# Batch 2's q and k through DMA transposes, on top of a reworked first and second batch, in a fused Nyström attention and MLP kernel

## The chip, the cores and the metric

The kernel runs on one core of one Trainium2 chip. The metric is the device time of one execution in microseconds, lower is better. Batches are numbered from 0, so the "third batch" of the change is batch 2. Unless a run is called slow, all times are of fast runs; a program on one core has no second die to compare with, so a run counts as slow when it lies over 1.5% above the fastest of its kernel.

## The reference

The inputs are q, k and v of 8 batches, 8 heads, 576 positions and 64 channels, and two MLP weights.

```python
q_lm = q.reshape(B, H, 32, 18, D).mean(axis=3)      # landmarks: segment means
k_lm = k.reshape(B, H, 32, 18, D).mean(axis=3)
A, Bm, C = sm(q, k_lm), sm(q_lm, k_lm), sm(q_lm, k) # softmax(a b^T / 8)
Z = Bm^T / (norm_1(Bm) * norm_inf(Bm) + 1e-6)       # per head, schematic
for _ in range(6):
    Z = 2 * Z - Z @ Bm @ Z                          # Newton steps for the inverse
x = A @ Z @ C @ v                                   # then [4608, 512]
out = relu(x @ w_in) ** 2 @ w_out                   # d_ff = 2048
```

## The kernel before

The kernel never forms x. It folds `Z C v` and `w_in` of a batch into one matrix `G`, so that the MLP's first product is `G^T A^T` (`mlp_in`), the second is `mlp_out`. While TensorE works on the MLP of batch b, the attention of batch b+1 is woven into its instruction stream. The order of each engine's instructions is fixed when the program is built.

This kernel's score matmuls read q and k with the channels on the partitions, that is, transposed. Batches below `DMA_T` do it with TensorE (36 transposes of 128 columns, the results then copied out of PSUM), later ones with DMA transposes:

```python
DMA_T = 3

def prepare(b, nms=("k", "q")):                     # cut
    ...
        nc.vector.tensor_copy(X[nm][:], raw)        # "cast": reorders heads and columns
        if b >= DMA_T:
            nc.sync.dma_start_transpose(X[nm + "T"]..., X[nm]...)
    if "k" in nms:
        ...
        if b >= DMA_T:
            nc.sync.dma_start_transpose(X["tT"][:], X["qkt"]...)   # the last 64 rows, "tails"
```

When a batch's cast may run is pinned to a point in the batch before it. For batches 3 to 7 this is the first Newton step of the batch before; for batch 2 it is later, after batch 1's `WT` (k) and the last copy of its `G` (q):

```python
for it in range(3):
    EY, ED, last = joint_step(EY, ED)
    if it == 0 and b > 1:
        X["kpin"] = X["qpin"] = last
...
last = nc.vector.tensor_copy(WT[:], wt[:])
if b == 1:
    X["kpin"] = last
for n in range(4):                                  # G, in four parts
    ...
        last = nc.vector.tensor_copy(dst, gg[:])    # every second part
        if b == 1:
            X["qpin"] = last
```

All loads but those of batch 0's q and k are issued by GpSimd on one queue, in this order: w_in, v of batch 0, q and k of batch 1, w_out, and so on.

The softmax here doesn't subtract the row's maximum and nothing guards it: scores larger than these inputs give would overflow.

Of the kernel before, what the change touches and what calls it, by code (L numbers as in the profile page):

```python
# [8 lines left out]
P = 128  # L9
# [8 lines left out]
H = 8  # L18
S = 576
D = 64  # L20
# [10 lines left out]
DMA_T = 3  # L31
# [3 lines left out]
def kernel(  # L35
# [97 lines left out]
    masked = band(mask4[:], [[32, 4]], 31, -1)  # L133
    blk_bf = const.tile([P, 4, M], BF16, name="blk_bf")
    nc.vector.tensor_copy(blk_bf[:], mask4[:, :].unsqueeze(2).to_broadcast([P, 4, M]))
# [37 lines left out]
    def prepare(b: int, nms=("k", "q")):  # L173

        X = loaded[b]
        for nm in nms:
            X[nm] = loads.tile([P, NC4, H, D], BF16, tag=nm + "nat", bufs=1, name="nat")
            X[nm + "T"] = attn.tile([P, NC4, NPAIR, P], BF16, tag=nm + "T", name="T")
            raw = X[nm + "raw"].rearrange("p h c d -> p c h d")
            if b == 0:  # L180
                for lo, hi in ((0, H // 2), (H // 2, H)) if nm == "q" else ((0, H),):
                    nc.vector.tensor_copy(X[nm][:, 0:2, lo:hi, :], raw[:, 0:2, lo:hi, :])
                    nc.scalar.copy(X[nm][:, 2:4, lo:hi, :], raw[:, 2:4, lo:hi, :])
                continue
# [10 lines left out]
    def warm(n):  # L195

        z = bds[1].rearrange("p a b c -> p (a b c)")
        for _ in range(n):
            nc.tensor.matmul(idle[:, 0:2 * P], lhsT=z[:, 0:P], rhs=z[:, 0:2 * P],
                             start=True, stop=True)  # L200

    def attention(b: int, R: dict):
# [6 lines left out]
        def transposed(nm, half):  # L209
            if not first:  # L210
                tps = ntile([P, 2, NPAIR, P], BF16)[:]
            else:
                tps = psum.tile([P, 4, NPAIR, P], BF16, tag="h", bufs=2, name="tps")[:, 0:2, :, :]
# [20 lines left out]
        def segment_means(ti, nm):  # L234
# [5 lines left out]
            for n, (p, c) in enumerate(order):  # L240
                src = X[nm][:, c, 2 * p:2 * p + 2, :] if c < NC4 else X["qkt"][:, 2 * p:2 * p + 2, :]
                nc.tensor.matmul(  # L242
                    means[:, ti, p, :],
                    lhsT=src.rearrange("p h d -> p (h d)"),
                    rhs=seg[:, c + (ti if c == NC4 else 0), :],
                    start=(n == 0 and (first or ti == 1)), stop=(c == NC4), skip_group_check=True,
                )
# [44 lines left out]
        def stationary(src, tag):  # L292

            if first:
# [3 lines left out]
                nc.vector.tensor_copy(res[:], src)  # L298
# [23 lines left out]
        def inverse_begin():  # L322
# [3 lines left out]
            cs = small.tile([P, 2], F32, tag="cs", name="cs")  # L326
            nc.vector.reduce_sum(cs[:], BB[:, 0, :, :], axis=AX.X)
            rows = small.tile([P, 2, M], F32, tag="rows", name="rows")
            nc.vector.transpose(rows[:], cs[:, :].unsqueeze(2).to_broadcast([P, 2, M]))
# [79 lines left out]
        ras = [small.tile([P, NC4 + 1, 4], F32, tag="ra", name="ra") for i in range(2)]  # L409
        rras = [small.tile([P, NC4 + 1, 4], F32, tag="rra", name="rra") for i in range(2)]  # L410
        parts = ((0, 3), (3, NC4 + 1)) if first else ((0, NC4 + 1),)

        def a_sums(i, part=0):
            lo, hi = parts[part]
            nc.vector.reduce_sum(ras[i][:, lo:hi, :],  # L415
                                 EA[:, i, lo:hi, :].rearrange("p c (h m) -> p c h m", m=M), axis=AX.X)
            if hi == NC4 + 1:
                nc.vector.reciprocal(rras[i][:], ras[i][:])

        def a_rows(i, part=0):  # L420
            lo, hi = parts[part]
# [3 lines left out]
                rras[i][:, lo:hi, :].unsqueeze(3).to_broadcast([P, hi - lo, 4, M]), ALU.mult)  # L425
# [13 lines left out]

        def c_values():  # L440

            cv = ntile([P, 2, D + 1])
            for qd in range(2):
                for c in range(NC4 + 1):
                    for lo, hi in ((0, D), (D, D + 1)):
                        for a in range(4):
                            h = 4 * qd + a
                            lh = EC[:, qd, c, :] if c < NC4 else ect[:, qd, :]
                            rv = (ones_bf[:] if lo else
                                  X["vm"][:, h, c, :] if c < NC4 else X["vt"][:, h, :])  # L450
                            nc.tensor.matmul(  # L451
                                cv[M * a:M * a + M, qd, lo:hi], lhsT=lh[:, M * a:M * a + M], rhs=rv,
                                start=(qd == 0 and c == 0 and lo == 0), stop=(c == NC4),
                                skip_group_check=True)
            rc2 = small.tile([P, 2], F32, tag="rc2", name="rc2")
            nc.vector.reciprocal(rc2[:], cv[:, :, D])
            nc.vector.tensor_tensor(cvb[:], cv[:, :, 0:D],
# [3 lines left out]
        if first:  # L461
            prepare(0, ("k",))
            warm(6)
            k0 = transposed("k", 0)
            k1 = transposed("k", 1)
            load_rest(dve(X["qkt"][:], X["qkt32"][:]))
            dve(*k0)
            act(*k1)
            segment_means(1, "k")
            transposed_tail()  # L470
            prepare(0, ("q",))
            warm(8)
# [3 lines left out]
            dve(*q0)  # L476
            q1 = transposed("q", 1)
            landmark_softmax()
            act(*q1)
            scores("k", 0)  # L480
            BT, ED = inverse_first(*inverse_begin())
# [37 lines left out]
        def aside():  # L519
            for f, *args in side.pop(0):  # L520
                f(*args)
            if first:
                warm(2)
# [215 lines left out]
```

## Time and profile before

| | before |
|---|---|
| median time | 273.28 us (3 runs), 273.21 us with the fourth |
| first MLP matmul | 24.64 us |
| first matmul of G of batch 1 | 51.67 us |
| from there to G of batch 2 | 30.71 us |
| batches after that | 31.37 and 28.16 us in turn |
| batch 2's first q scores | 69.38 us |

The rows of this table come from the timeline view. First the page's busy shares, and three rows of its 40 slices (each slice 6.8 us; a digit is a busy share in tenths; PEclk is the clock granted to TensorE):

```profile
PE 254.2 (94%) x3051; PEld 150.2 (56%) x3051; DVE 174.9 (65%) x497; ACT 157.6 (58%) x274; POOL 42.7 (16%) x66
...
PE   2978799999999999999999999999999999999994
...
PEclk9999999999999999999999999999999999999999
DMA  7999999999699979997599929994821011211032
```

TensorE is full from the sixth slice on. The DMA row is at 7 or 9 for the first ten slices, about 67 us. The windows view with the columns span, busy time of each engine, clock, DMA share and GB/s says the same of TensorE in figures:

```profile
60.00:80.00 20.00, 19.50 (x259) 12.53 (x258) 17.10 (x54) 14.01 (x25) 3.77 (x5) 1.00 1.05 128
100.00:120.00 20.00, 19.90 (x266) 11.07 (x265) 14.34 (x36) 11.36 (x19) 3.42 (x4) 1.00 1.27 148
```

The chain of work that ended last (start, length, what) goes through DMA at the start:

```profile
9.19 7.26 DMA vm<-in_v_dram
16.73 14.90 DMA raw<-in_q_dram
```

The timeline of the kernel before has the first MLP matmul, and batch 2's first q scores, which follow a TensorE transpose and wait for nothing:

```profile
24.64 0.67 PE L601 MATMUL h<-AT,G 128*128 128x288 bf16 x4 [0.30 <-ACT G L579]
...
68.24 0.39 PE L226 MATMUL n<-ident_bf,qkt 128*128 128x128 bf16 x4
...
69.38 0.40 PE L390 MATMUL n<-bd_83,T 128*128 128x64 bf16 x8
```

The view of one tile, asked for the transposed q and k, gives the time of DMA transposes from issue to landing. This is all ten of them, and then the two of batch 7, issued when no load was left in the queues:

```profile
DMA to landing us min/median/max: 5.1/10.7/20.5
...
DMA to landing us min/median/max: 5.1/5.2/5.3
```

In this kernel the same transpose took 5.1 to 5.3 us with no load in the queues and 9.6 to 20.5 us, two to four times as much, in batches 3 to 6, beside loads.

### The profile page before, as it was taken

The page shows a single profiled execution, that of the slowest core. Times are in us where ns is not written, and L with a number is a line of the kernel's source. Part 1 is how long each engine was busy: PE and PEld are TensorE (multiplying, and loading weights), DVE is VectorE, ACT ScalarE, POOL GpSimd, SP SyncE. Part 2 cuts the span into 40 slices and gives each one's busy share as a digit, 9 for nine tenths or more (in the row PEclk, how much of TensorE's full clock was granted, in tenths as well). Part 3 has the DMA queues.
Part 4 walks back from the last instruction along what each step waited for, and adds up shares of the span by engine and source line. Part 5 has one row for each costly group of instructions (what it writes and reads, how often), then busy time and mean ns, then how long its engine had stood idle before and what let it go on. Part 6 is the DMA issues. An engine that isn't in the chain of part 4 may idle for free.

```text
span 270.4 us, 7294 instructions
## 1 busy us (share of the span) xinstructions
PE 254.2 (94%) x3051; PEld 150.2 (56%) x3051; DVE 174.9 (65%) x497; ACT 157.6 (58%) x274; POOL 42.7 (16%) x66
## 2 busy tenths in 40 slices
PE   2978799999999999999999999999999999999994
PEld 1844565466654665556644665466645665466444
DVE  4687788758794569647974669548964859545100
ACT  2555687366935677267926676467836674577211
POOL 3744333310420202202220220200000000000000
PEclk9999999999999999999999999999999999999999
DMA  7999999999699979997599929994821011211032
GB/s 207 229 203 198 203 205 190 209 207 144 83 160 123 186 107 137 199 159 105 113 157 153 177 61 155 174 149 80 176 61 62 18 41 41 78 41 40 19 98 79
DMA packets 69793, 35.34 MB, mean 131 GB/s; under 512 B 37376, under 2 KB 64256, under 8 KB 69760
## 3 DMA queue, kind: packets, MB, share of 16 engines
q0 software_dynamic: 37696, 17.17, 54.5%
q1 hardware_dynamic: 26816, 8.39, 22.4%
q10 hardware_dynamic: 5248, 9.31, 11.3%
q8 instruction: 24, 0.39, 0.6%
q14 instruction: 9, 0.07, 0.1%
HBM read 36.70 MB, written 9.44 MB: 171 GB/s over the span
## 4 chain that ended last, share of the span: by engine, by line
PE 69%; DVE 15%; DMA 10%; ACT 3%; issue 1%; SPq 0%; POOL 0%; DVEq 0%
PE ops L630 21%; PE h L601 16%; PE n L630 9%; DMA raw<-in_q_dram 6%; DVE gT L608 4%; PE g L573 3%; DMA vm<-in_v_dram 3%; DVE ra L415 2%; PE n L314 2%; DMA qkt_94<-in_q_dram 2%; ACT r L607 2%; PE n L451 2%; PE n L242 2%; PE n L390 1%; DVE an L422 1%; PE n L432 1%
## 5 line engine op out<-in xcount | busy, mean ns | idle before, releaser
L607 ACT ACTIVATE r<-h 128x576 bf16<-128x576 f32 x128 | 81.9, 652 | 33.4 <-PE h L601 30.4
L601 PE MATMUL h<-AT,G 128*128 128x288 bf16 x512 | 83.1, 286 | 1.2 <-ACT r L607 0.8
L630 PE MATMUL ops<-w_out_bf,gT 128*128 128x512 bf16 x304 | 83.2, 379 | 0.1
L608 DVE TENSOR_TENSOR gT<-r 128x576 bf16<-128x576 bf16 x128 | 57.4, 452 | 39.2 <-ACT r L607 38.1
L630 PEld LDWEIGHTS <-gT 128*128 128x128 bf16 x592 | 53.6, 98 | 40.5 <-issue 6.4
L601 PEld LDWEIGHTS <-G 128*128 128x128 bf16 x512 | 45.5, 97 | 21.6 <-issue 2.4
L630 PE MATMUL n<-w_out_bf,gT 128*128 128x512 bf16 x112 | 29.6, 380 | 0.0
L587 DVE CAST G<-g 128x1024 bf16<-128x1024 f32 x14 | 17.1, 1225 | 13.2 <-PE g L573 13.2
L585 ACT CAST G<-g 128x1024 bf16<-128x1024 f32 x14 | 14.2, 1012 | 9.5 <-PE g L573 9.1
L639 ACT COPY o_sb<-ops 128x512 f32<-128x512 f32 x19 | 11.1, 585 | 4.5 <-PE ops L630 4.4
L436 ACT COPY AT<-n 128x576 bf16<-128x576 bf16 x9 | 5.7, 638 | 13.5 <-PE n L432 11.1
L314 PEld LDWEIGHTS <-ED 128*128 128x128 bf16 x84 | 6.7, 97 | 12.2 <-DVE ED L305 8.4
L390 PEld LDWEIGHTS <-T 128*128 128x128 bf16 x256 | 11.3, 98 | 3.7
L422 DVE TENSOR_TENSOR an<-EA,rra 128x640 bf16<-128x640 f32 (+2 forms) x18 | 13.3, 740 | 0.0
L415 DVE TENSOR_REDUCE ra<-EA 128x20 f32<-128x640 f32 (+2 forms) x18 | 13.0, 721 | 0.0
L84 POOL DMA_DIRECT2D qkt<-in_k_dram x7 | 4.8, 690 | 46.7 <-PE n L252 30.1
L106 POOL DMA_DIRECT2D vm<-in_v_dram x8 | 7.1, 881 | 32.1 <-PE n L451 27.4
L242 PEld LDWEIGHTS <-nat 128*128 128x128 bf16 x256 | 8.7, 97 | 5.1 <-DVE nat L185 2.3
L96 POOL DMA_DIRECT2D raw<-in_k_dram x7 | 6.6, 936 | 29.3 <-DVE ED L305 18.6
L394 ACT ACTIVATE EA<-n 128x512 f32<-128x512 f32 x16 | 9.7, 607 | 1.8 <-PE n L390 1.8
L185 DVE COPY nat<-raw 128x2048 bf16<-128x2048 bf16 x14 | 9.4, 686 | 1.6 <-DMA raw<-in_q_dram 0.9
L394 ACT ACTIVATE EC<-n 128x512 bf16<-128x512 f32 x16 | 9.7, 604 | 1.2 <-PE n L390 1.1
(185 smaller groups left out, 322.6 us busy)
## 6 DMA issues: line engine op xcount, KB each, us to landing
out_dram<-o_sb ACTq DMA_DIRECT2D x31, 256.0 KB, 4.0
vm<-in_v_dram POOLq DMA_DIRECT2D x8, 512.0 KB, 14.7
raw<-in_k_dram POOLq DMA_DIRECT2D x7, 512.0 KB, 10.5
raw<-in_q_dram POOLq DMA_DIRECT2D x7, 512.0 KB, 13.8
w_in_bf<-in_moe_w_in_dram POOLq DMA_DIRECT2D x4, 512.0 KB, 10.2
w_out_bf<-in_moe_w_out_dram POOLq DMA_DIRECT2D x4, 512.0 KB, 16.2
out_dram<-o_sb ACTq DMA_DIRECT2D x9, 128.0 KB, 2.4
raw<-in_k_dram SPq DMA_DIRECT2D x1, 1024.0 KB, 5.5
```

The source lines that it names most:

```text
L242: nc.tensor.matmul(means[:, ti, p, :], lhsT=src.rearrange("p h d -> p (h d)"), rhs=seg[:, c + (ti if c == NC4 else 0), :], start=(n == 0 a ...
L314: nc.tensor.matmul(res[a:a + w, qd, :], lhsT=diagonal[a:a + w, qd, :], rhs=moving(qd)[a:a + w], start=True, stop=True)
L390: nc.tensor.matmul(sc[:, c, j, :, :], lhsT=X[nm + "T"][:, c, p, :], rhs=BD[:, 1 if nm == "q" else 0, p, 0:64], start=True, stop=True)
L394: nc.scalar.activation((EA if nm == "q" else EC)[:, qd, 0:NC4, :], sc.rearrange("p c j i m -> p c (j i m)"), AF.Exp, scale=SCALE)
L415: nc.vector.reduce_sum(ras[i][:, lo:hi, :], EA[:, i, lo:hi, :].rearrange("p c (h m) -> p c h m", m=M), axis=AX.X)
L422: nc.vector.tensor_tensor(an[:, i, lo:hi, :].rearrange("p c (h m) -> p c h m", m=M), EA[:, i, lo:hi, :].rearrange("p c (h m) -> p c h m", ...
L585: nc.scalar.copy(dst, gg[:])
L587: last = nc.vector.tensor_copy(dst, gg[:])
L601: last = nc.tensor.matmul(h[:, j, 0:HALF], lhsT=G[:, qd, f * P:(f + 1) * P], rhs=AT[:, qd, j * HALF:(j + 1) * HALF], start=(qd == 0), stop ...
L607: nc.scalar.activation(r.rearrange("p (j t) -> p j t", j=2), h[:, :, 0:HALF], AF.Relu)
L608: return nc.vector.tensor_tensor(gT[:, f, o:o + S], r[:], r[:], ALU.mult)
L630: mark[:] = [nc.tensor.matmul(ops, lhsT=gT[:, f, t * P:t * P + P], rhs=w_out_bf[:, f, i * n:i * n + n], start=(f == 0), stop=(f == NF - 1))]
```

## The change

Its intent: start the first MLP matmuls sooner, keep the second batch from blocking them, and relieve TensorE of batch 2's transposes, which the DMA engines do "for free" in all later batches. The diff, cut to its core:

```diff
-DMA_T = 3
+DMA_T = 2
@@ row sums of C: 10 full matmuls instead of 40 column-tiled ones
-                    for lo, hi in ((0, D), (D, D + 1)):
-                        for a in range(4):
-                            ...
+            for qd in range(2):
+                for c in range(NC4 + 1):
+                    nc.tensor.matmul(cv[:, qd, D:D + 1], lhsT=c_of(qd, c), rhs=ones_bf[:],
+                                     start=False, stop=(c == NC4), skip_group_check=True)
@@ first batch (many lines cut): weight loads follow the k cast, q is cast in halves,
@@ k's scores come later, fewer idle matmuls, G's first part is copied in halves
+            load_rest(X["cast"])
+            prepare(0, ("q",), ((0, H // 2),))
-            load_rest(dve(X["qkt"][:], X["qkt32"][:]))
@@ second batch: k transposed with the segment means, steps spread by a table
+            if b == 1:
+                for half, evac in ((0, dve), (1, act)):
+                    evac(*transposed("k", half))
+                    yield
+        early = [0, 0, 0, 0, 0, 0, 1, 2, 3, 3, 4, 5, 7, 9, 12, half]
-            if (b, f) == (0, 2):
-                loaded[0]["qpin"] = square
+            if b == 0 and f in (4, 8):
+                loaded[0][("kpin", "qpin")[f // 8]] = square
                 prepare_next(1)
```

In the built program two orders move that the diff doesn't show. On the load queue, batch 2's v now comes before its k and q. On SyncE, which issues the transposes, batch 3's tail transpose stands before batch 2's k transpose.

More of the change, by code (lines that the diff above doesn't have):

```diff
@@ L133 @@
     masked = band(mask4[:], [[32, 4]], 31, -1)
+    blk = const.tile([P, 4, M], F32, name="blk")
+    nc.vector.tensor_copy(blk[:], mask4[:, :].unsqueeze(2).to_broadcast([P, 4, M]))
     blk_bf = const.tile([P, 4, M], BF16, name="blk_bf")
-    nc.vector.tensor_copy(blk_bf[:], mask4[:, :].unsqueeze(2).to_broadcast([P, 4, M]))
+    nc.vector.tensor_copy(blk_bf[:], blk[:])
     ones_bf = const.tile([P, 1], BF16, name="ones_bf")
@@ L171, in ntile, with prepare @@
         return psum.tile(shape, dt, tag="n", bufs=3, name="n")
-    def prepare(b: int, nms=("k", "q")):
+    def prepare(b: int, nms=("k", "q"), halves=((0, H),)):
         X = loaded[b]
         for nm in nms:
-            X[nm] = loads.tile([P, NC4, H, D], BF16, tag=nm + "nat", bufs=1, name="nat")
-            X[nm + "T"] = attn.tile([P, NC4, NPAIR, P], BF16, tag=nm + "T", name="T")
+            if nm not in X:
+                X[nm] = loads.tile([P, NC4, H, D], BF16, tag=nm + "nat", bufs=1, name="nat")
+                X[nm + "T"] = attn.tile([P, NC4, NPAIR, P], BF16, tag=nm + "T", name="T")
             raw = X[nm + "raw"].rearrange("p h c d -> p c h d")
             if b == 0:
-                for lo, hi in ((0, H // 2), (H // 2, H)) if nm == "q" else ((0, H),):
+                for lo, hi in halves if nm == "q" else ((0, H),):
                     nc.vector.tensor_copy(X[nm][:, 0:2, lo:hi, :], raw[:, 0:2, lo:hi, :])
-                    nc.scalar.copy(X[nm][:, 2:4, lo:hi, :], raw[:, 2:4, lo:hi, :])
+                    X["cast"] = nc.scalar.copy(X[nm][:, 2:4, lo:hi, :], raw[:, 2:4, lo:hi, :])
                 continue
@@ L193, in prepare, with warm, in_turn @@
                 nc.sync.dma_start_transpose(X["tT"][:], X["qkt"].rearrange("p h d -> p (h d)"))
-    def warm(n):
+    def warm(n, width=512):
         z = bds[1].rearrange("p a b c -> p (a b c)")
         for _ in range(n):
-            nc.tensor.matmul(idle[:, 0:2 * P], lhsT=z[:, 0:P], rhs=z[:, 0:2 * P],
+            nc.tensor.matmul(idle[:, 0:width], lhsT=z[:, 0:P], rhs=z[:, 0:width],
                              start=True, stop=True)
+    mark, begin, front = [], [], []
+    def in_turn():
+        return tc.issue_after(front[0].ins) if front else nullcontext()
     def attention(b: int, R: dict):
@@ L212, in transposed @@
             else:
-                tps = psum.tile([P, 4, NPAIR, P], BF16, tag="h", bufs=2, name="tps")[:, 0:2, :, :]
+                if half == 0:
+                    X["tps"] = psum.tile([P, 4, NPAIR, P], BF16, tag="h", bufs=2, name="tps")
+                tps = X["tps"][:, 2 * half:2 * half + 2, :, :]
             for i in range(2):
@@ L239, in segment_means @@
                            (0, x[1] // 2, x))
-            for n, (p, c) in enumerate(order):
-                src = X[nm][:, c, 2 * p:2 * p + 2, :] if c < NC4 else X["qkt"][:, 2 * p:2 * p + 2, :]
-                nc.tensor.matmul(
-                    means[:, ti, p, :],
-                    lhsT=src.rearrange("p h d -> p (h d)"),
-                    rhs=seg[:, c + (ti if c == NC4 else 0), :],
-                    start=(n == 0 and (first or ti == 1)), stop=(c == NC4), skip_group_check=True,
-                )
+            with in_turn() if b == 1 else nullcontext():
+                for n, (p, c) in enumerate(order):
+                    src = X[nm][:, c, 2 * p:2 * p + 2, :] if c < NC4 else X["qkt"][:, 2 * p:2 * p + 2, :]
+                    nc.tensor.matmul(
+                        means[:, ti, p, :],
+                        lhsT=src.rearrange("p h d -> p (h d)"),
+                        rhs=seg[:, c + (ti if c == NC4 else 0), :],
+                        start=(n == 0 and (first or ti == 1)), stop=(c == NC4), skip_group_check=True,
+                    )
             if not first and ti == 1:
@@ L297, in stationary @@
                 res = newt.tile([P, 2, M], BF16, tag="U", name="U")
-                nc.vector.tensor_copy(res[:], src)
+                nc.scalar.copy(res[:], src)
                 return res[:]
@@ L325, in inverse_begin @@
             BT = stationary(btc[:], "BT")
-            cs = small.tile([P, 2], F32, tag="cs", name="cs")
-            nc.vector.reduce_sum(cs[:], BB[:, 0, :, :], axis=AX.X)
-            rows = small.tile([P, 2, M], F32, tag="rows", name="rows")
-            nc.vector.transpose(rows[:], cs[:, :].unsqueeze(2).to_broadcast([P, 2, M]))
+            if first:
+                rows = ntile([P, 2, M])
+                nc.tensor.matmul(rows.rearrange("p a m -> p (a m)"),
+                                 lhsT=blk.rearrange("p a m -> p (a m)"),
+                                 rhs=BB[:, 1, :, :].rearrange("p a m -> p (a m)"),
+                                 start=True, stop=True)
+            else:
+                cs = small.tile([P, 2], F32, tag="cs", name="cs")
+                nc.vector.reduce_sum(cs[:], BB[:, 0, :, :], axis=AX.X)
+                rows = small.tile([P, 2, M], F32, tag="rows", name="rows")
+                nc.vector.transpose(rows[:], cs[:, :].unsqueeze(2).to_broadcast([P, 2, M]))
             n1 = small.tile([P, 2], F32, tag="n1", name="n1")
@@ L407, in tails, with a_sums, a_recip, a_quad_sums @@
                 tl[P - TAIL:P, :, 0, :], AF.Exp, scale=SCALE)
-        ras = [small.tile([P, NC4 + 1, 4], F32, tag="ra", name="ra") for i in range(2)]
-        rras = [small.tile([P, NC4 + 1, 4], F32, tag="rra", name="rra") for i in range(2)]
-        parts = ((0, 3), (3, NC4 + 1)) if first else ((0, NC4 + 1),)
-        def a_sums(i, part=0):
-            lo, hi = parts[part]
-            nc.vector.reduce_sum(ras[i][:, lo:hi, :],
-                                 EA[:, i, lo:hi, :].rearrange("p c (h m) -> p c h m", m=M), axis=AX.X)
-            if hi == NC4 + 1:
-                nc.vector.reciprocal(rras[i][:], ras[i][:])
-        def a_rows(i, part=0):
-            lo, hi = parts[part]
+        one, two = slice(0, 1), slice(1, 2)
+        ra = small.tile([P, 2, NC4 + 1, 4], F32, tag="ra", name="ra")
+        rra = small.tile([P, 2, NC4 + 1, 4], F32, tag="rra", name="rra")
+        def a_sums(lo, hi, quads=slice(0, 2)):
+            nc.vector.reduce_sum(ra[:, quads, lo:hi, :],
+                                 EA[:, quads, lo:hi, :].rearrange("p q c (h m) -> p q c h m", m=M),
+                                 axis=AX.X)
+        def a_recip(i):
+            nc.vector.reciprocal(rra[:, i, :, :], ra[:, i, :, :])
+        def a_quad_sums(i):
+            a_sums(0, NC4 + 1, slice(i, i + 1))
+            a_recip(i)
+        def a_rows(i, lo=0, hi=NC4 + 1):
             nc.vector.tensor_tensor(
@@ L424, in a_rows @@
                 EA[:, i, lo:hi, :].rearrange("p c (h m) -> p c h m", m=M),
-                rras[i][:, lo:hi, :].unsqueeze(3).to_broadcast([P, hi - lo, 4, M]), ALU.mult)
+                rra[:, i, lo:hi, :].unsqueeze(3).to_broadcast([P, hi - lo, 4, M]), ALU.mult)
         def a_transposed(i):
@@ L438, in attention, with c_of, c_scaled @@
         cvb = small.tile([P, 2, D], BF16, tag="cvb", name="cvb")
+        cvs = []
         def c_values():
             cv = ntile([P, 2, D + 1])
+            cvs.append(cv)
+            def c_of(qd, c):
+                return EC[:, qd, c, :] if c < NC4 else ect[:, qd, :]
             for qd in range(2):
                 for c in range(NC4 + 1):
-                    for lo, hi in ((0, D), (D, D + 1)):
-                        for a in range(4):
-                            h = 4 * qd + a
-                            lh = EC[:, qd, c, :] if c < NC4 else ect[:, qd, :]
-                            rv = (ones_bf[:] if lo else
-                                  X["vm"][:, h, c, :] if c < NC4 else X["vt"][:, h, :])
-                            nc.tensor.matmul(
-                                cv[M * a:M * a + M, qd, lo:hi], lhsT=lh[:, M * a:M * a + M], rhs=rv,
-                                start=(qd == 0 and c == 0 and lo == 0), stop=(c == NC4),
-                                skip_group_check=True)
+                    for a in range(4):
+                        h = 4 * qd + a
+                        nc.tensor.matmul(
+                            cv[M * a:M * a + M, qd, 0:D], lhsT=c_of(qd, c)[:, M * a:M * a + M],
+                            rhs=X["vm"][:, h, c, :] if c < NC4 else X["vt"][:, h, :],
+                            start=(qd == 0 and c == 0), stop=(c == NC4), skip_group_check=True)
+            for qd in range(2):
+                for c in range(NC4 + 1):
+                    nc.tensor.matmul(cv[:, qd, D:D + 1], lhsT=c_of(qd, c), rhs=ones_bf[:],
+                                     start=False, stop=(c == NC4), skip_group_check=True)
+            if not first:
+                c_scaled()
+        def c_scaled():
+            cv, = cvs
             rc2 = small.tile([P, 2], F32, tag="rc2", name="rc2")
             nc.vector.reciprocal(rc2[:], cv[:, :, D])
+            if first:
+                for qd in range(2):
+                    nc.scalar.activation(cvb[:, qd, :], cv[:, qd, 0:D], AF.Copy,
+                                         scale=rc2[:, qd:qd + 1])
+                return
             nc.vector.tensor_tensor(cvb[:], cv[:, :, 0:D],
@@ L462, in attention @@
             prepare(0, ("k",))
-            warm(6)
+            load_rest(X["cast"])
+            warm(3)
             k0 = transposed("k", 0)
             k1 = transposed("k", 1)
-            load_rest(dve(X["qkt"][:], X["qkt32"][:]))
-            dve(*k0)
-            act(*k1)
+            dve(X["qkt"][:], X["qkt32"][:])
+            kept = dve(*k0)
+            prepare(0, ("q",), ((0, H // 2),))
             segment_means(1, "k")
+            prepare(0, ("q",), ((H // 2, H),))
             transposed_tail()
-            prepare(0, ("q",))
-            warm(8)
+            warm(3)
             segment_means(0, "q")
@@ L475, in attention @@
             landmark_scores()
-            dve(*q0)
             q1 = transposed("q", 1)
             landmark_softmax()
-            act(*q1)
-            scores("k", 0)
-            BT, ED = inverse_first(*inverse_begin())
-            scores("q", 0)
-            side = [[(scores, "q", 1), (a_sums, 0, 0)],
-                    [(tails,), (a_sums, 1, 0)],
-                    [(scores, "k", 1), (a_sums, 0, 1)],
-                    [(a_sums, 1, 1), (a_rows, 0, 0), (warm, 2)],
-                    [(a_rows, 0, 1), (c_values,)],
-                    [(a_transposed, 0), (a_rows, 1, 0)],
-                    [(a_rows, 1, 1), (warm, 2)],
-                    [(a_transposed, 1)]]
-        else:
-            for ti, nm in ((1, "k"), (0, "q")):
-                segment_means(ti, nm)
-                yield
+            other = dve(*q0)
+            tc.declare_no_dep(act(*q1).ins, other.ins, reason="other banks")
+            tc.declare_no_dep(act(*k1).ins, kept.ins, reason="other banks")
+            warm(2)
+            begun = inverse_begin()
+            warm(1)
+            BT, ED = inverse_first(*begun)
+            scores("q", 0)
+            warm(1)
+            side = [[(scores, "q", 1), (warm, 1, 256), (a_sums, 0, 2, one)],
+                    [(tails,), (warm, 1, 256), (a_sums, 2, 4, one)],
+                    [(scores, "k", 0), (warm, 1, 256), (a_sums, 4, 5)],
+                    [(scores, "k", 1), (warm, 1), (a_sums, 0, 2, two)],
+                    [(warm, 1), (a_recip, 0), (a_rows, 0, 0, 3)],
+                    [(a_rows, 0, 3, 5), (a_sums, 2, 4, two), (c_values,)],
+                    [(c_scaled,), (a_transposed, 0), (a_recip, 1)],
+                    [(a_rows, 1)]]
+        else:
+            segment_means(1, "k")
+            yield
+            if b == 1:
+                for half, evac in ((0, dve), (1, act)):
+                    evac(*transposed("k", half))
+                    yield
+            segment_means(0, "q")
+            yield
             landmark_scores()
@@ L507, in attention @@
                 yield
-                dve(*transposed("k", 0))
-                yield
-                act(*transposed("k", 1))
-                yield
+                if b > 1:
+                    dve(*transposed("k", 0))
+                    yield
+                    act(*transposed("k", 1))
+                    yield
                 transposed_tail()
@@ L514, in attention @@
             side = [[(scores, "q", 0)], [(scores, "q", 1)], [(tails,)],
-                    [(a_sums, 0), (scores, "k", 0)], [(scores, "k", 1), (a_rows, 0)],
-                    [(a_sums, 1), (a_transposed, 0)], [(c_values,)],
+                    [(a_quad_sums, 0), (scores, "k", 0)], [(scores, "k", 1), (a_rows, 0)],
+                    [(a_quad_sums, 1), (a_transposed, 0)], [(c_values,)],
                     [(a_rows, 1)], [(a_transposed, 1)]]
@@ L521, in aside @@
                 f(*args)
-            if first:
-                warm(2)
         if not first:
@@ L545, in attention @@
             yield
-            aside()
+            if it == 0 or not first:
+                aside()
             yield
@@ L555, in attention @@
         WT = small.tile([P, 2, P], BF16, tag="WT", name="WT")
-        last = nc.vector.tensor_copy(WT[:], wt[:])
+        if first:
+            aside()
+            nc.scalar.copy(WT[:], wt[:])
+        else:
+            last = nc.vector.tensor_copy(WT[:], wt[:])
         if b == 1:
@@ L559, in attention @@
         if first:
-            warm(3)
+            warm(2)
         yield
         for n in range(4):
-            with tc.issue_after(mark[0].ins) if n == 2 and mark else nullcontext():
+            with in_turn() if first and n >= 2 else (
+                    tc.issue_after(mark[0].ins) if n == 2 and mark else nullcontext()):
                 if first and n >= 1:
@@ L578, in attention @@
             if first:
-                lo = nc.scalar.copy(dst[:, 0, :], g[0])
-                last = nc.vector.tensor_copy(dst[:, 1, :], g[1])
-                tc.declare_no_dep(last.ins, lo.ins, reason="other columns and banks")
-                if n == 0:
-                    X["kpin"] = last
+                for c in ((0, 256), (256, 512)) if n == 0 else ((0, 512),):
+                    if c[0]:
+                        a_transposed(1)
+                    lo = nc.scalar.copy(dst[:, 0, slice(*c)], g[0][:, slice(*c)])
+                    last = nc.vector.tensor_copy(dst[:, 1, slice(*c)], g[1][:, slice(*c)])
+                    tc.declare_no_dep(last.ins, lo.ins, reason="other columns and banks")
             elif n % 2 == 0:
@@ L589, in attention @@
                     X["qpin"] = last
-            if n % 2:
+            if first and n == 0 or n == 3:
+                R[b] = (AT, G)
+            if n % 2 or first and n == 2:
                 yield
-        R[b] = (AT, G)
-    mark, begin = [], []
     def mlp_in(b, f, AT, G, gT):
@@ L603, in mlp_in @@
                                         start=(qd == 0), stop=(qd == 1))
+        front[:] = [last]
         if (b, f) == (0, 9):
@@ L660 @@
                                      mybir.EngineType.Activation}):
-        for _ in attention(0, R):
-            pass
+        start = attention(0, R)
+        while 0 not in R:
+            next(start)
     gT, tiles = None, iter(())
@@ L687, in attend @@
                 prepare_next(b + 2)
-        late = 3 if b == 0 else 0
+        early = [0, 0, 0, 0, 0, 0, 1, 2, 3, 3, 4, 5, 7, 9, 12, half]
         prepare_next(b + 1)
@@ L692 @@
             square = mlp_in(b, f, AT, G, gT)
-            if (b, f) == (0, 2):
-                loaded[0]["qpin"] = square
+            if b == 0 and f in (4, 8):
+                loaded[0][("kpin", "qpin")[f // 8]] = square
                 prepare_next(1)
+            if (b, f) in ((0, 1), (0, 3)):
+                advance(start, 1)
             advance(tiles, 3 if b % 2 == 0 else 2)
-            attend((f + 1 - late) * half // (NF - late))
+            attend(early[f] if b == 0 else (f + 1) * half // NF)
         for _ in tiles:
```

## The prediction

> **What bounds the kernel now.** From about 40 us on, TensorE's instruction stream: the windows view gives PE busy 19.5 to 19.97 of every 20 us from 60 to 240 us at clock 1.00; 512- and 288-column matmuls start 0.216 and 0.122 us apart. Before that it is start-up latency. The chain of waits runs through DMA for the first 32 us: v of batch 0 (7.3 us), then q of batch 1 (14.9 us). The timeline has the first MLP matmul at 24.6 us and TensorE waiting on batch 1's k and q until 32.4. The page's DMA row is near full until 65 us, so the in-order load queue, about 196 KB/us, paces all arrivals.
>
> **What the change does.**
> 1. Start: weight loads follow the k cast (7.3 us) instead of the tail cast (8.1); q cast in halves, k scores later, fewer idle matmuls, split G copies. Against it, a 0.69 us q copy now stands on VectorE between softmax and Newton. Estimate: first MLP matmul 1 us earlier, and 1.5 us more because batch 1's segment means no longer block mlp_in: -2.5.
> 2. C's row sums: 40 column-tiled matmuls become 10 full ones per batch; from start-to-start intervals (8 and 26 ns[...]) -0.1 per batch: -0.9.
> 3. Batch 2 loses 36 TensorE transposes at 56 ns: -2.0. Its copies on VectorE and ScalarE (about 4 us) were off the path.
> 4. Batch 2 gains three DMA transposes. Those of q and k took 5.1 to 5.3 us in the last batch, with the queues nearly empty, but 9.6 to 20.5 us from issue to landing under load; from k's cast to q's landing 18 to 25 us.
>
> Steps 1 to 3 are on the critical path: -5.4, giving 268 alone.
>
> **Step 4 makes a new wait.** Transposes of batches 3 to 7 start half a batch ahead, pinned to the previous batch's first Newton step. Batch 2's stay pinned to batch 1's WT and G copies, 51 to 54 us. The instruction order makes it worse: batch 2's v is now loaded before its k and q (3.7 us), and on SyncE batch 3's tail transpose stands before batch 2's k transpose, which so waits for batch 3's tail loads, about 55 us. From there the DMA engines have about 20 us of work (estimate: transposes 12, batch 3's loads 9, an output, less overlap)[...]: transposes take two to four times as long beside loads. So q's transpose lands at 70 to 76 us. TensorE, in order, reaches batch 2's first q scores 9 us of work after G of batch 1 (about 51), near 61; before, they ran at 69.4. It stalls about 12 us (6 to 16), which nothing later makes up.
>
> **Predicted:** 273.3 - 5.4 + 12 = 280 us, range 273.5 to 285. Faster by over 2%: 0.08; within: 0.31; slower: 0.61.
>
> **What would show it.** First MLP matmul near 23.5, G of batch 1 near 51; no TensorE transposes of batch 2's q and k; one TensorE gap of 6 to 16 us between 58 and 77 us, ended by q's DMA transpose in the waits view; afterwards batches of about 29.7 us as before.
>
> **What would make it wrong.** Transposes that get a larger share and land by 63: then 268 to 270, possibly faster by over 2%. A start-up gain of 4 us or more would turn the loss into "same". A late q load that also holds back G's copies would add to the loss.

The first is a term of step 2's sum: 40 times 8 ns less 10 times 26 ns is 0.06 us a batch, about 0.5 us in 8 batches, and the cut term brought it to the 0.1 a batch and 0.9 in all that stand there. The forecast's sum: -2.5 - 0.9 - 2.0 = -5.4, and 273.3 - 5.4 + 12 = 280 us. The estimate's 12 and 9 us fit the trace: two transposes of 5.2 us and one of a quarter of their size, and 1728 KB of loads at the text's 196 KB/us (the DMA view of the kernel before, 20 to 60 us, has 7.48 MB on the load queue, 187 KB/us).

## More of the kernel before

The two transposes of batch 7, which overlap, moved 1.05 MB from 191.4 to 197.2 us, about 181 GB/s, and by themselves took 94% of the time of all 16 (DMA view with that window). In the first nine slices of the page, mostly loads, the DMA engines moved 190 to 229 GB/s.

## The result, and the profile after

The changed kernel takes 282.01 us (281.0 to 283.71, 4 runs) against 273.21 us (272.81 to 273.67, 4 runs). The ratio is 1.0328, 95% interval 1.0275 to 1.0381: slower. All ratios here are the mean time of one kernel's fast runs over that of the other's in the same rounds, so not quite the ratio of the medians.

| | before | after |
|---|---|---|
| first MLP matmul | 24.64 us | 25.15 us |
| G of batch 1 | 51.67 us | 52.01 us |
| from there to G of batch 2 | 30.71 us | 39.87 us |
| from there to the end | 188.01 us | 188.46 us |

Nearly the whole loss, 9.2 of the 9.95 us between the two profiles, lies between two points, G of batch 1 and G of batch 2. The page's rows for the changed kernel (a slice is now 7.0 us):

```profile
PE 250.3 (89%) x2711; PEld 148.8 (53%) x2757; DVE 174.7 (62%) x490; ACT 157.7 (56%) x278; POOL 43.1 (15%) x66
...
PE   2888999872499999999999999999999999999995
...
PEclk9997999997599999999999999999999999999999
DMA  7999999999569994996199989991541010101222
```

TensorE is busy for 3.9 us less than before, and has a hole in the tenth and eleventh slices (63 to 77 us). Under that hole the clock row drops to 7 and 5. (The 7 further left, in the fourth slice, is a stretch of 3.4 us at half clock, 22.70 to 26.12 us, in the start. Such a stretch came in some executions of several of these kernels, e2 and e7 for instance, and not in others; batch 0's k also landed 0.6 us later in this execution. That is why this profile shows no earlier start, while e1's does.) The waits view names what TensorE waited for (total, times, longest):

```profile
PE n L408 <- DMA T<-nat: 9.1, 1, 9.1
...
PE h L656 <- DVE G L642: 1.5, 1, 1.5
PE g L627 <- DVE G L642: 1.0, 1, 1.0
```

L408 is the scores. The timeline of TensorE shows the hole itself. The matmul at 73.99 us is the first of batch 2's q scores:

```profile
64.22 0.21 PE L325 MATMUL n<-btc,BT 128*128 128x32 bf16 x2 [0.16 <-DVE BT L316]
64.28 0.65 PE L656 MATMUL h<-AT,G 128*128 128x288 bf16 x4
73.99 0.61 PE L408 MATMUL n<-bd,T 128*128 128x64 bf16 x8 [9.06 <-DMA T<-nat]
```

And the chain that ended last holds both DMA transfers that matter, batch 2's q load and its transpose:

```profile
42.64 14.28 DMA raw<-in_q_dram
...
65.69 8.26 DMA T<-nat
```

The q transpose was issued at 65.69 us and landed at 73.95; TensorE went on 40 ns later. Before that, VectorE had twice waited for a late load in order to cast it, and each time its next instruction was a copy of G: for batch 2's k (landed at 53.38 us; TensorE's wait of 1.0 us) and for its q (landed at 56.92 us; the wait of 1.5 us).

Windows of 6 us around the hole, with the columns as above:

```profile
61.00:67.00 6.00, 3.69 (x27) 2.01 (x26) 4.62 (x20) 3.92 (x8) 1.14 (x2) 1.00 1.42 181
67.00:73.00 6.00, 0.00 (x0) 0.00 (x0) 0.00 (x0) 0.00 (x0) 0.00 (x0) 0.51 1.38 186
73.00:79.00 6.00, 5.01 (x38) 3.28 (x40) 2.43 (x7) 2.33 (x4) 0.68 (x1) 0.64 0.09 20
```

From 67 to 73 us no engine computes anything, and only DMA runs. The DMA share falls to 0.09 in the window in which the transpose lands: q's transpose was among the last of everything that the DMA engines had to do. The clock column holds a cost that I had not foreseen: the trace has it at one half from 67.08 to 77.32 us. The first 7 us of that fall into the hole, but the last 3.3 us into work, which cost about 1.7 us (half of it; an estimate). The eight matmuls at 73.99 us show it: they took 0.61 us, the same eight in the kernel before 0.40. On the chain that ended last, the four MLP matmuls of 288 columns that follow at 74.60 us took 0.96 us; four at 78.04, with the clock back, 0.49.

### The profile page after: what moved, and what is told of

Same layout as the page of the kernel before. It is cut to its first block, busy times and chain, and to the rows that moved or that the text cites. A ratio compares the mean times of both kernels' runs of the same rounds, so it can differ in the third digit from the quotient of the medians.

```text
span 280.3 us, 6675 instructions
## 1 busy us (share of the span) xinstructions
PE 250.3 (89%) x2711; PEld 148.8 (53%) x2757; DVE 174.7 (62%) x490; ACT 157.7 (56%) x278; POOL 43.1 (15%) x66
## 4 chain that ended last, share of the span: by engine, by line
PE 62%; DVE 11%; DMA 10%; ACT 10%; issue 5%; DVEq 0%; ACTq 0%
PE ops L686 29%; PE h L656 14%; DMA raw<-in_q_dram 5%; ACT r L663 5%; PE n L686 5%; DVE gT L664 3%; DMA T<-nat 3%; PE g L627 2%; ACT G L640 2%; DMA raw<-in_k_dram 2%; PE n L253 2%; DVE ra L432 2%; PE n L454 2%; PE n L325 1%; PE n L408 1%
## 5 line engine op out<-in xcount | busy, mean ns | idle before, releaser
L686 PE MATMUL ops<-w_out_bf,gT 128*128 128x512 bf16 (+1 forms) x451 | 114.9, 373 | 2.3
L663 ACT ACTIVATE r<-h 128x576 bf16<-128x576 f32 x128 | 82.8, 655 | 31.3 <-PE h L656 27.5
L656 PE MATMUL h<-AT,G 128*128 128x288 bf16 x512 | 84.0, 289 | 3.2 <-DVE G L642 1.5
L695 ACT COPY o_sb<-ops 128x512 f32<-128x512 f32 (+1 forms) x29 | 16.8, 578 | 37.1 <-PE ops L686 37.1
L686 PE MATMUL n<-w_out_bf,gT 128*128 128x512 bf16 x98 | 28.7, 380 | 0.3
L408 PE MATMUL n<-bd,T 128*128 128x64 bf16 x256 | 13.2, 195 | 9.1 <-DMA T<-nat 9.1
L408 PEld LDWEIGHTS <-T 128*128 128x128 bf16 x256 | 11.6, 99 | 14.5 <-DMA T<-nat 9.4
L330 DVE SCALAR_TENSOR_TENSOR EY<-EY,n 128x128 bf16<-128x128 bf16 x24 | 6.8, 283 | 12.7 <-PE n L325 12.6
L325 PEld LDWEIGHTS <-ED 128*128 128x128 bf16 x84 | 7.4, 99 | 11.5 <-DVE ED L316 4.9
L432 DVE TENSOR_REDUCE ra<-EA 128x20 f32<-128x640 f32 (+1 forms) x19 | 13.0, 698 | 0.4
L627 PE MATMUL g<-w_in_bf,WT 64*32 64x512 bf16 x232 | 9.6, 389 | 2.0 <-DVE G L642 1.0
## 6 DMA issues: line engine op xcount, KB each, us to landing
w_in_bf<-in_moe_w_in_dram POOLq DMA_DIRECT2D x4, 512.0 KB, 10.8
```

What stands on the lines that cost most here:

```text
L325: nc.tensor.matmul(res[a:a + w, qd, :], lhsT=diagonal[a:a + w, qd, :], rhs=moving(qd)[a:a + w], start=True, stop=True)
L408: nc.tensor.matmul(sc[:, c, j, :, :], lhsT=X[nm + "T"][:, c, p, :], rhs=BD[:, 1 if nm == "q" else 0, p, 0:64], start=True, stop=True)
L432: nc.vector.reduce_sum(ra[:, quads, lo:hi, :], EA[:, quads, lo:hi, :].rearrange("p q c (h m) -> p q c h m", m=M), axis=AX.X)
L627: nc.tensor.matmul(g[i][M * p:M * p + M, :], lhsT=WT[64 * i:64 * i + 64, i, M * p:M * p + M], rhs=w_in_bf[64 * i:64 * i + 64, p, n * 512:n ...
L656: last = nc.tensor.matmul(h[:, j, 0:HALF], lhsT=G[:, qd, f * P:(f + 1) * P], rhs=AT[:, qd, j * HALF:(j + 1) * HALF], start=(qd == 0), stop ...
L663: nc.scalar.activation(r.rearrange("p (j t) -> p j t", j=2), h[:, :, 0:HALF], AF.Relu)
```

## The experiments

Twelve kernels ran. Edits are against the changed kernel unless said otherwise. All gave correct results.

### The two halves of the change apart

**e1_rework_only** and, with more rounds, **e12_rework_again**:

```diff
-DMA_T = 2
+DMA_T = 3
```

> The changed kernel with batch 2's q and k transposed by TensorE again (the constant back at 3); the rework of the first two batches stays. Theory L (batch 2's DMA transposes come too late, and that alone is the loss): no TensorE wait on a DMA transpose, time 271 to 274 us, so 8 to 11 us below the changed kernel, and G of batch 1 again near 52. Rival R (the rework is itself the loss: half clock at its start, v loaded before k and q): 278 us or more.

> The kernel of e1_rework_only unchanged, more rounds: 0.1 to 0.5 per cent below before (the prediction had the rework at 1.2 per cent below, 3.4 of 5.4 us).

Measured: 272.55 us, ratio 0.9974 (0.9924 to 1.0025), and with more rounds 272.21 us, 0.9965 (0.9938 to 0.9992). TensorE waits for no transpose. The way from G of batch 1 to G of batch 2 is 29.96 us instead of 39.87. So the rework is not the loss, and rival R falls. But it gains about 1 us, not 3.4.

**e2_dma_only**, an edit of the kernel before:

```diff
-DMA_T = 3
+DMA_T = 2
```

> The kernel before with DMA transposes from batch 2 on and nothing else. The load order here has k and q before v again, so they land near 48.4 and 51.0 as before. Theory L: TensorE waits for q's transpose here too, 4 to 8 us instead of 9, as k's cast is about 3 us earlier; time 277 to 281. Rival R: within 1 us of before, 272 to 274.

Measured: 282.95 us, ratio 1.0354 (1.0295 to 1.0412). The one constant gives the whole loss. The wait is 9.9 us, not the 4 to 8 that I expected:

```profile
PE n L390 <- DMA T<-nat: 9.9, 1, 9.9
```

Batch 2's k and q landed at 48.60 and 51.33 us, 5 us sooner than in the changed kernel, and q's transpose still landed at 74.70. So earlier loads alone didn't help. It is no test of issuing earlier, though: batch 3's tail transpose stands in front on SyncE here too, and q's transpose was issued at 66.79 us, later than the 65.69 of the changed kernel. (The text for e9, below, counts e2 among the kernels that issued earlier; that is a slip.)

### Only one of the two

**e3_k_only**: k of batch 2 by DMA, q and the tails by TensorE; **e8_k_only_again** is the same for more rounds.

```diff
-DMA_T = 2
+DMA_T = 3
+DMA_K = 2
-            if b >= DMA_T:
+            if b >= (DMA_K if nm == "k" else DMA_T):
                 nc.sync.dma_start_transpose(
...
-                if b > 1:
-                    dve(*transposed("k", 0))
-                    yield
-                    act(*transposed("k", 1))
-                    yield
```

(The number of steps of batch 2's attention goes from 28 to 26 with it.)

> The changed kernel, but only k of batch 2 goes through the DMA transpose; its q and its tails go through TensorE. k's scores come some 7 us of work after q's, and k's transpose has no tail transpose in front of it. Theory L (what hurts is q's landing, behind k's and behind a tail): the wait of 9.1 us is gone or under 2 us, time 271 to 274.5, at most 1 us from the rework alone. Rival C (any DMA transposes at that time hurt, through contention with the loads): 276 us or more.

> The kernel of e3_k_only unchanged, for more rounds beside e7_old_sums and the kernel before: 271 to 272.5 us, 0.2 to 0.7 per cent below before.

Measured: 271.58 us, ratio 0.9955 (0.9903 to 1.0006), then 271.16 us, 0.9925 (0.9912 to 0.9938; one slow run of 276.5 us left out). No wait on a transpose shows. The one k transpose took 12.9 us to land in the second profile (52.41 to 65.29 us), far more than 5, but its scores come late enough. Against the rework alone (0.9965) this is 0.4%, about 1.1 us; 16 TensorE transposes at 56 ns are 0.9. But e8 and e12 ran in different rounds and their intervals touch; in the rounds that they share, e3 is only 0.2% (about 0.5 us) below e1, with intervals that overlap. So the gain is likely, and its size is not shown. This is the fastest kernel, 0.75% below the kernel before in e8's rounds, 0.45% in e3's.

**e11_before_k_only**: the same edit on the kernel before, without the rework.

> The kernel before, with only batch 2's k through the DMA transpose and no rework of the first two batches. It tells how much of e3_k_only's 0.75 per cent is the transpose: 16 TensorE transposes less are 0.9 us if the stretch is TensorE-bound, and no wait on the transpose may show. Expected 272 to 273 us, 0 to 0.4 per cent below before; above before by more than 0.5 per cent would say that even one transpose delays the loads enough to hurt.

Measured: 273.19 us, ratio 1.0009 (0.9979 to 1.004): just outside what was expected, and no gain is shown. So a gain from the single transpose is likely with the rework and not seen without it; why was not followed up.

### The hole filled with idle work

**e4_fill**: 40 matmuls that nobody needs, placed just before batch 2's first q scores.

```diff
+        if b == 2:
+            filler = ntile([P, 512])
+            z = bds[1].rearrange("p a b c -> p (a b c)")
+            with tc.issue_after(front[0].ins):
+                for _ in range(40):
+                    fill = nc.tensor.matmul(filler[:], lhsT=z[:, 0:P], rhs=z[:, 0:512],
+                                            start=True, stop=True)
         if not first:
-            aside()
+            with tc.issue_after(fill.ins) if b == 2 else nullcontext():
+                aside()
```

> The changed kernel with 40 matmuls of 512 columns that nobody needs put in TensorE's order just before batch 2's first q scores (8.6 us of TensorE work at full clock). Theory L: they run inside the wait, so the time does not grow by 8.6 us; and since TensorE is then not idle, the granted clock should stay at 1.00 after the gap instead of 0.5 for 10 us, so the time should fall by 1 to 2 us, to 280 to 281. If the gap were TensorE work hidden from the profile, the time would grow to about 290.

Measured: 280.71 us, ratio 1.0278 (1.0232 to 1.0325). The 40 added matmuls, 8.80 us of TensorE's timeline (64.47 to 73.27 us), made the kernel no slower; it even came out 1.3 us faster, as the two ratios to the kernel before also have it (1.0278 against 1.0328). What remained of the wait, and the window of the former hole:

```profile
PE n L408 <- DMA T<-nat: 0.5, 1, 0.5
```

```profile
67.00:73.00 6.00, 6.00 (x30) 2.65 (x27) 0.00 (x0) 0.00 (x0) 0.00 (x0) 1.00 1.38 203
```

The clock is 1.00 in this window and in the next two, to 85 us. So the hole was a pure wait, and the clock loss after it was a separate cost, which went away here, with TensorE busy in the hole. The intervals of the two ratios just fail to separate (1.0275 to 1.0381 and 1.0232 to 1.0325 overlap), so the size, 1 to 2 us, rests on the clock records more than on the times.

### Issued earlier: does it help?

**e5_sp_order**: on SyncE, batch 3's tail transpose comes after batch 2's q transpose.

```diff
-                nc.sync.dma_start_transpose(
+                X[nm + "dma"] = nc.sync.dma_start_transpose(
...
+                with tc.issue_after(loaded[2]["qdma"].ins) if b == 3 else nullcontext():
-                nc.sync.dma_start_transpose(X["tT"][:], ...)
+                    nc.sync.dma_start_transpose(X["tT"][:], ...)
```

> The changed kernel, but on the queue that issues transposes batch 3's tail transpose comes after batch 2's q transpose instead of in front of batch 2's k transpose. Theory L: k's transpose is issued with its cast, near 54 instead of 59.5, q's near 57.5 instead of 65.7; under the same load 13 and some 14 us to landing, so q lands near 70 to 71.5 and the wait shrinks from 9.1 to 5 to 7 us; time 278 to 280. If only the load of the DMA engines mattered and not the order of issue: no change, 281 to 283.

**e6_all_earlier**: the same, and batch 2's k and q are loaded before its v, and cast one step earlier.

```diff
+            with tc.issue_after(loaded[2]["qload"].ins) if b == 0 else nullcontext():
-            load_v(b + 2, loaded[b + 2])
+                load_v(b + 2, loaded[b + 2])
...
             y, v, last = newton_step(y, UD, it == 1)
+            if b == 1 and it == 0:
+                X["kpin"] = last
...
         if b == 1:                      # at WT
-            X["kpin"] = last
+            X["qpin"] = last
```

> As e5_sp_order, and batch 2's k and q are loaded before its v again (landing near 48.5 and 51 instead of 52 and 55.5), with their casts pinned one step earlier (a Newton step and WT of batch 1). Theory L: k's transpose is issued near 50 to 51, q's near 53, q lands near 64 to 68; the wait is 0 to 4 us, G's copies no longer wait for the q load (1.0 and 1.5 us less)[...]; time 272 to 276.

Both missed what theory L expected; e5 fell on the other outcome written down for it. e5 took 282.25 us (1.0329, 1.0312 to 1.0347), e6 280.57 us (1.0274, 1.0241 to 1.0308). In e5, k's transpose was issued at 52.99 instead of 59.47 us and q's at 58.27 instead of 65.69. In e6, q's was issued at 54.91. The chains of e5 and then of e6 show what became of q's lead (e6's profile is of the slowest of its four runs, 282.27 us):

```profile
58.27 15.05 DMA T<-nat
```

```profile
54.91 18.22 DMA T<-nat
```

Issued 7.4 us and 10.8 us earlier than in the changed kernel, it took 15.05 and 18.22 us instead of 8.26, and landed at 73.3 and 73.1 instead of 73.95. In e5 the wait did shrink, from 9.1 to 7.7 us, but the time didn't: TensorE waited longer for G's copies (2.2 and 0.7 us), and the clock was at one half twice, from 58.56 to 61.97 and from 68.80 to 79.04 us. In e6 the other loads paid: batch 3's q landed at 76.84 us instead of 67.98. And since e6 has no wait on G's copies to speak of, TensorE only got to the scores sooner and waited longer there, 10.1 us:

```profile
PE n L409 <- DMA T<-nat: 10.1, 1, 10.1
```

So a late issue of q's transpose isn't the cause: five kernels with issue times from 54.91 to 66.79 us have it land between 73.1 and 74.7. k's transpose, which goes first, did gain from its lead: it landed at 65.78 us in e5 and 63.55 in e6 instead of 72.35. TensorE needs q first, however; in the kernel before, k's scores come 5.2 us after q's (74.60 and 69.38 us). Issuing q's transpose before k's is the order that was not tried, and the record can't say how much of the wait it would have taken away.

### The competing loads taken away

**e9_hold_loads**: as e6, and batch 3's k, q and v loads wait until batch 2's q transpose has landed.

```diff
+                if b == 3 and nm == "k":
+                    tc.add_manual_dep(
+                        one.ins, loaded[2]["qdma"].ins.name,
+                        mybir.DependencyInfo(mybir.DependencyClass.Sync,
+                                             mybir.DependencyReason.DATA),
+                        reason="transposes first")
...
+            with tc.issue_after(loaded[b + 2]["qload"].ins) if b < 2 else nullcontext():
-            with tc.issue_after(loaded[2]["qload"].ins) if b == 0 else nullcontext():
                 load_v(b + 2, loaded[b + 2])
```

> As e6_all_earlier, and the loads of batch 3's k, q and v are not issued before batch 2's q transpose has landed. e2, e5 and e6 issued the transposes up to 10 us earlier, yet q's landed at 73 to 75 us in all of them, so theory L (issued too late) does not suffice. Theory C now: the DMA engines have a fixed amount of work from about 49 to 74 us, and q's transpose lands when nearly all of it is done, whatever the order of issue. If C holds, taking some 9 us of loads out of its way brings q's transpose to 62 to 66 us and the wait from 10.1 to 0 to 2 us; time 270 to 275 (batch 3's loads then land some 10 us later and may cost 1 or 2 us). If the transposes are slow by themselves in that stretch: q's landing stays at 70 or more and the time at 279 or more.

Measured: 276.84 us, ratio 1.0177 (1.0143 to 1.0212). The chain of e9 and then two lines of its TensorE timeline:

```profile
54.26 8.40 DMA T<-nat
...
64.27 7.50 DMA raw<-in_q_dram
```

```profile
62.71 0.41 PE L415 MATMUL n<-bd,T 128*128 128x64 bf16 x8 [0.52 <-DMA T<-nat]
...
71.00 1.12 PE L663 MATMUL h<-AT,G 128*128 128x288 bf16 x4 [3.33 <-ACT r L670]
```

With the loads out of its way, q's transpose, issued within 0.7 us of the time in e6, took 8.40 us instead of 18.22. The wait of 10.1 us is down to 0.5, and the intervals of the two ratios don't overlap (1.0241 to 1.0308 for e6). Theory C fits: in e6 the DMA share was 1.37 to 1.69 in each 6 us window from 49 to 73 us, in e9 it fell to 0.81 from 61 to 67. And the transposes took the time of the same 16 engines as the loads: in the changed kernel, from 65.7 to 73.9 us, the queue of the transposes had 85% of it, that of the loads 31% and that of the outputs 15% (DMA view; packets overlap). The time is above the expected 270 to 275, because the bill came later: batch 3's k and q now landed at 69.12 and 71.77 us, VectorE waited for them to cast them, ScalarE could not go on without VectorE, and TensorE stood for 3.33 us behind ScalarE (then with the clock at one half from 69.81 to 76.64 us). This profile is of e9's fastest run, 275.27 us; what the others, up to 279.04 us, lost beyond that isn't shown. Whoever went first in that stretch, someone else was late.

### Two side questions

**e10_k_only_q_first**: e3_k_only with batch 2's k and q loaded before its v (the edit of e6 at `load_v`).

> The kernel of e3_k_only with batch 2's k and q loaded before its v, as the kernel before has it. VectorE's cast of q then need not hold back the copies of G: the wait of the MLP matmuls on G's copies, 1.5 us in e3_k_only, should be under 0.5 us, and the time 270 to 271, 0.2 to 0.5 per cent below e3_k_only.

Measured: 273.83 us, ratio 1.0026 (1.0004 to 1.0049), a miss. The wait on VectorE's copies of G did go, but batch 3's k landed at 67.92 instead of 64.95 us (e8), and the Newton steps of batch 2 waited 3.6 us for VectorE instead. This is the stretch in which the changed kernel has a DMA share of 1.34 to 1.71 (49 to 73 us; e10's own was not asked for), with the lateness moved elsewhere.

**e7_old_sums**: e3_k_only with the row sums of C as the kernel before computes them.

> The kernel of e3_k_only with the row sums of C as they were before (40 column-tiled matmuls a batch instead of 10 full ones). The prediction had the new form 0.1 us a batch faster, so this would be 0.7 to 0.9 us slower than e8_k_only_again. The traces so far say otherwise: batches 3 to 7 took 28.28 and 31.38 us with the new form and 28.16 and 31.37 with the old, so I now expect this one to be 0.2 to 0.7 us faster.

Measured: 273.2 us, ratio 0.9993 (0.9976 to 1.001), so 0.7% slower than e8, where I had expected it faster. But the batches from 3 on differ by only 0.05 to 0.06 us each (31.44, 28.34, 31.43 us against 31.38, 28.29, 31.37). Most of the difference is batch 2's, 31.32 against 29.88 us, where the built order of instructions changed as well and a wait of 1.4 us on VectorE appeared. The trace has VectorE there behind batch 3's q, which landed at 71.00 us instead of 69.27 (e8), so this is e10's lateness again. The new row sums are worth some 0.06 us a batch; why that load was later stays open.

## Why the prediction was right, and where it was not

- **The new wait: right.** TensorE stood once, for 9.06 us, between 58 and 77 us, ended by q's DMA transpose, which landed at 73.95 us (predicted 70 to 76). e1 and e2 show that the constant alone makes it. What TensorE reached at 61 us in the prediction it reached at 64.9: 1.0 us because G of batch 1 came at 52.01 instead of 51, 2.5 because late loads also held back G's copies, and 0.4 is left over. The prediction had named the copies as something that would add to the loss. That made the hole shorter, but not the loss smaller.
- **Why q's transpose lands late: half right.** The prediction gave two reasons: late issue (pins, load order, the tail transpose in front) and full DMA engines. e5 removed a part of the first and e6 most of it, and q's landing moved by only 0.6 and 0.8 us; e9 removed the second as well, and all but 0.5 us of the wait was gone. The estimate of "about 20 us of work" for the DMA engines from 55 us on, which gave 70 to 76, was the part that carried it. How the engines divide their time between queues no run here shows; the times do show what the loads cost a transpose: 18.22 us beside them (e6), 8.40 without most of them (e9), 5.1 to 5.3 with none (batch 7 in the kernel before).
- **Step 3 of the sum, 36 transposes fewer, -2.0: fits the sum below, not shown alone.** 16 of them, 0.9 us by the same count, came out at 1.1 us (e8 against e12), 0.5 (e3 against e1) and nothing (e11), all within or near the noise.
- **Step 1, the rework, -2.5: mis-sized.** The first MLP matmul did come about 1 us sooner (23.73 and 23.38 us in e1 and e12). The further 1.5 us, "because batch 1's segment means no longer block mlp_in", were not there: from the first MLP matmul to G of batch 1 e1 took 27.34 us, the kernel before 27.03. The whole rework, row sums included, measured 0.35% (e12), just under 1 us.
- **Step 2, row sums, -0.9: mis-sized.** From G of batch 2 to the end, the kernel before took 188.01 us, the changed one 188.46, e1 188.63. Replacing 40 column-tiled matmuls that start 8 ns apart by 10 full ones that start 25 to 26 ns apart saved next to nothing (e7: 0.06 us a batch).
- **Not in the prediction: the clock.** About 1.7 us, from 73.99 to 77.32 us at half clock (e4). What the traces show of it: in the changed kernel the clock fell to one half 2.15 us into the wait (1.8 to 3.1 us in e5, e6 and e9), and in e5 it had already done so once around a wait of 2.2 us. Full clock came back 3.3 us after the restart here, and 3.9 to 5.7 us after it in e2, e5, e6 and e9. What sets these times is not shown. I looked at the clock of the kernel before, which is 1.00, and did not ask what a hole would do to it.

The sum, from e1 to the changed kernel, for the way from G of batch 1 to G of batch 2: 9.1 us of wait, 1.3 more of waiting for G's copies (2.5 against 1.2), 1.7 of clock, less 2.0 for the transposes: 10.1, measured 9.9 (39.87 - 29.96). That the prediction of 280 came near 282 is partly luck. Its gain of 5.4 should have been about 3, and it left 1.3 us of copies and 1.7 of clock out of the sum: all three made it too low, by 5.4 us together. Its wait of 12 us, measured as 9.1, made it 2.9 too high and hid about half of that. So +12 was right only for the sum of wait, copies and clock.

## What to carry to other kernels

Here, work moved from TensorE to DMA cost TensorE no wait where the consumer came late enough (batch 2's k in e8, 12.9 us to landing), and 9.06 us where it did not (batch 2's q): look at the DMA row of the very stretch in which it will run, not at the duration it has elsewhere in the trace (5.1 to 5.3 us in batch 7). In the full stretch, issuing q's transpose up to 10.8 us earlier made it land at most 0.8 us earlier, as long as the loads ran beside it; taking loads out of its way helped, and then those were late. And count a hole on TensorE longer than it looks: in these traces the clock came back 3.3 to 5.7 us after the work did.
